# Linear attention and a multiplicative FFN on one core: the product with kv in quarters of the array

## The chip, the core and the metric

The kernel runs on one NeuronCore of a Trainium2 chip. TensorE (PE in the profile) multiplies: it holds a block of weights of up to 128 rows by 128 columns and streams the other operand through it, into PSUM, the accumulator memory. VectorE (DVE), ScalarE (ACT) and GpSimd (POOL) work on vectors; SyncE (SP) and POOL issue the DMAs. SBUF is the on-chip memory of 128 partitions.

The metric is the device time of one execution in microseconds (us), the median of several. An engine runs its own instructions in the order in which they were written; engines wait for each other by semaphores.

## The reference

For 8 batches and 8 heads, with 576 positions and 64 channels a head, the attention is linear; its result, with heads side by side as 512 channels, is the x of a feed-forward network on 4608 tokens.

```python
q_s = exp(q - max(q, -1)); q_s = q_s / (sum(q_s, -1) + 1e-09)
k_s = exp(k - max(k, 2));  k_s = k_s / (sum(k_s, 2) + 1e-09)
kv = einsum('bhsd,bhse->bhde', k_s, v)
attn = einsum('bhsd,bhde->bhse', q_s, kv)
x = attn.transpose(0, 2, 1, 3).reshape(4608, 512)
a = x @ w1                      # 512 x 1024
b = x @ w2
h = a * b @ w3                  # 1024 x 1024
out = h @ w_out                 # 1024 x 512
```

## The kernel before, in words

**Layout.** A partition holds a group g (0 or 1) of four heads and a block of 9 positions: partition g*64 + p has positions 9p to 9p+8 of heads 4g to 4g+3. Heads are handled in pairs: pair hp (0 or 1) of group g has the heads 4g+2hp and 4g+2hp+1, and i (0 or 1) tells them apart. 512 of the 576 positions of a batch (8 of each 9) are its main block, and make one chunk of the FFN; the remaining 64 positions of all 8 batches are collected in `xtail`, the ninth chunk.

**Attention of batch b.** The steps have these names: `kmx` (DVE, maximum of k over positions in a partition, L300 or the tree L306 to L311), `kmt` (TensorE transposes it, L317), `mx` (DVE, L322 and L324), `kmb` (TensorE transposes back, L332), `cb` (ACT copies it to SBUF, L337), `ksub` (L341, on POOL from batch 1 on), `kexp` (ACT, L349), `vc` (v to f16, L354), `kv` (TensorE, L365: 36 matmuls over 64 rows, g taking turns, with a column of ones that gives the sum of k). `kv2` (DVE, L372 to L376) takes the reciprocal of that sum and scales kv: the 128x128 product of a pair holds the two heads' kv on its diagonal 64x64 blocks and products of unlike heads off it, and a mask of ones and zeros, multiplied in, clears the latter. For q: `qmx` (DVE, L383), `qsub` (L387, POOL), `qexp` (ACT, L394), `qsm` (DVE, L400), `qeps` (ACT, L404), `qrc` (DVE, L408), `qn` (L413, POOL), `qt` (TensorE transposes, three groups of six, L422) and `qT` (ACT copies them to SBUF, L427). `xm` (L436) multiplies: for each pair and each g one full 128x128 by 128x512 matmul, into one PSUM tile; `xs` (ACT, L441) copies it to x, scaled. `xt` (L448) and `xts` (L453) do the same for the 64 tail positions, all four in one PSUM tile. The rows of x stand in the order pair, g, i; the loads of w1 and w2 pick their rows to fit.

**FFN of chunk c.** w3 is folded with w_out first (`w3t` L260, `w3T` L264, `pf` L269, `W3O` L273). Then for each of 8 blocks of 128 columns: `up` 1 and `up` 0 (TensorE, L531, four matmuls each, with w2 and with w1), `bs` (ACT, L537, copies the one out), `ab` (DVE, L542, multiplies the other with it). Four `down` (TensorE, L548, eight matmuls each) and `os` (ACT, L553) end the chunk, and SP stores it.

**What sets the order.** A planner (class `Plan`) does a list schedule when the kernel is built: each step has an engine, a length written by hand, the steps that it needs, and the PSUM or SBUF ring that it takes a buffer from; the planner always takes the step with the most work behind it among those that can start within 0.2 us. Its order is the order of the instructions. The rings: `pab` (4 PSUM banks, for `up`), `po` (2, for `down`), and `att` (2, for all of the attention: kmt, kmb, kv which takes both, qt, xm, xt). A step that takes a buffer waits for the evictions of the step that had it. `slack` adds 1 us to what a TensorE step of the attention assumes of its inputs.

**Loads.** SP loads k, q and v batch by batch, two buffers each; that of k of batch 1 waits for a load of w1 so that weights come first. POOL's queue loads the weights, converting them to f16.

The order of TensorE in the stretch that the prediction walks through is, before (batch numbers in brackets): `down`s of chunk 0, kv[1], down, qt[1] three times, kmt[2], xm[1] four times, kmb[2], then up 1 of chunk 1.

Of the kernel before, what the change touches and what calls it, by code (L numbers as in the profile page):

```python
# [9 lines left out]
F32 = mybir.dt.float32  # L10
# [113 lines left out]
def kernel(  # L124
# [15 lines left out]
    P = 128  # L140
# [31 lines left out]
    def p_att(shape, dtype, name):  # L172
        return att_pool.tile(shape, dtype, tag="att", name=name)
# [10 lines left out]
    ident16 = konst.tile([P, P], F16)  # L184
    ident32 = konst.tile([P, P], F32)
    epst = konst.tile([P, 1], F32)
    mask = konst.tile([P, P], F32)
    pace = konst.tile([P, 1], F32)
    make_identity(nc, ident16)
    make_identity(nc, ident32)  # L190
    dve.memset(epst, EPS)
    dve.memset(mask, 0.0)
    dve.memset(mask[0:64, 0:64], 1.0)
    dve.memset(mask[64:128, 64:128], 1.0)
    for t in v16buf:
        dve.memset(t[:, :, :, 128:129], 1.0)
    xtail = konst.tile([P, N_CT, B * HALF], F16)
# [38 lines left out]
    for n, which, dst in (("w2", moe_w2, w2sb), ("w1", moe_w1, w1sb)):  # L236
        for hp in range(NHP):
            for i in range(2):
                row = (4 * hp + 2 * i) * D
                w_load((n, hp, i), dst[i * HALF:(i + 1) * HALF, 2 * hp:2 * hp + 2, :],  # L240
                       which[row:row + 2 * D, :].rearrange("(g e) f -> e g f", g=G))

    def load(name, src, b, needs, after, wait):
        t = inbuf[name][b % 2]
# [39 lines left out]
    def attention(b):  # L284
# [84 lines left out]
        def kv2(gg):  # L369
            ps = st["pkv", b, gg]  # L370
            rc = work.tile([P, NHP], F32, tag="rc", name="rc")
            dve.tensor_scalar_add(out=rc, in0=ps[:, :, 128], scalar1=EPS)  # L372
            dve.reciprocal(out=rc, in_=rc)
            for hp in range(NHP):
                t = work.tile([P, P], F16, tag="kv2", name="kv2", bufs=8)
                dve.scalar_tensor_tensor(out=t, in0=ps[:, hp, 0:128], scalar=rc[:, hp:hp + 1],  # L376
                                         in1=mask, op0=ALU.mult, op1=ALU.mult)
                st["kv2", b, hp, gg] = t

        def qmx(hp):  # L380
            if ("qm", b) not in st:
# [46 lines left out]
                out=st["qT", b][:, n * BLK:(n + 1) * BLK, :, :].rearrange("p n g c -> p (n g c)"),  # L428
                in_=st["qtp", b, n].rearrange("p n c -> p (n c)"))

        def xm(hp, gg):
            ct = 2 * hp + gg
            if ("x", b) not in st:
                st["x", b] = work.tile([P, N_CT, MAIN], F16, tag="x", name="x", bufs=NX)
            st["px", b, ct] = p_att([P, NM, HALF], F32, "px")
            nc.tensor.matmul(st["px", b, ct], lhsT=st["kv2", b, hp, gg],  # L436
                             rhs=st["qT", b][:, hp * NJ:hp * NJ + NM, gg, :],
                             start=True, stop=True)

        def xs(ct):  # L440
            nc.scalar.mul(out=st["x", b][:, ct, :],  # L441
                          in_=st["px", b, ct].rearrange("p j c -> p (j c)"), mul=SC)

        def xt():
            st["pxt", b] = p_att([P, N_CT, HALF], F32, "pxt")
            for hp in range(NHP):
                for gg in range(G):
                    nc.tensor.matmul(st["pxt", b][:, 2 * hp + gg, :], lhsT=st["kv2", b, hp, gg],  # L448
                                     rhs=st["qT", b][:, hp * NJ + NM, gg, :],
                                     start=True, stop=True)  # L450

        def xts():
            nc.scalar.mul(out=xtail[:, :, b * HALF:(b + 1) * HALF], in_=st["pxt", b], mul=SC)  # L453

        def A(*a, **k):
            plan.add(*a, lead=LEAD, **k)
# [20 lines left out]
        A(("kv", b), "PE", 1.15, kv, [("kexp", b, hp) for hp in hps] +  # L477
          [("vc", b, hp) for hp in hps] + [("xt", b - 2)] * old, takes="att", slots=2, slack=SLACK)
        for gg in range(G):
            A(("kv2", b, gg), "DVE", 0.95, lambda gg=gg: kv2(gg),  # L480
              [("kv", b)], gives=[("kv", b)])
        for hp in hps:
            A(("qmx", b, hp), "DVE", 1.34, lambda hp=hp: qmx(hp), [("q", b)])
# [12 lines left out]
              [("xt", b - 2)] * old, takes="att", slack=SLACK)  # L496
            A(("qT", b, n), "ACT", 0.8, lambda n=n: qT(n), [("qt", b, n)], gives=[("qt", b, n)])
        for hp in hps:
            for gg in range(G):
                ct = 2 * hp + gg  # L500
                A(("xm", b, ct), "PE", 0.22, lambda hp=hp, gg=gg: xm(hp, gg),
                  [("kv2", b, gg)] + [("qT", b, n) for n in range((hp * NJ) // BLK,
                                                                   (hp * NJ + NM - 1) // BLK + 1)] +
                  [("up", 0, b - NX, N_FT - 1) for _ in range(1) if b >= NX], takes="att",
                  slack=SLACK)
                A(("xs", b, ct), "ACT", 0.6, lambda ct=ct: xs(ct), [("xm", b, ct)],
                  gives=[("xm", b, ct)])
        A(("xt", b), "PE", 0.2, xt, [("xm", b, ct) for ct in range(N_CT)], takes="att", slack=SLACK)
        A(("xts", b), "ACT", 0.4, xts, [("xt", b)], gives=[("xt", b)])

    NX = 3
    LEAD = 18.0
# [9 lines left out]
    def chunk(c):  # L522
        def x():
            return st["x", c] if c < B else xtail

        def up(fb, one):
            def mm():
                st["p", one, fb] = p_ab()
                w = (w1sb, w2sb)[one]
                for ct in range(N_CT):  # L530
                    nc.tensor.matmul(st["p", one, fb], lhsT=w[:, ct, fb * P:(fb + 1) * P],  # L531
                                     rhs=x()[:, ct, :], start=(ct == 0), stop=(ct == N_CT - 1))
# [12 lines left out]
        def down(tb):  # L545
            st["po", tb] = p_o()
            for ft in range(N_FT):
                nc.tensor.matmul(st["po", tb], lhsT=st["ab", c][:, ft, tb * P:(tb + 1) * P],  # L548
                                 rhs=W3O[:, ft, :], start=(ft == 0), stop=(ft == N_FT - 1))

        def os(tb):
            st["osb", tb] = work.tile([P, C], F32, tag="osb", name="osb", bufs=4)
            nc.scalar.copy(out=st["osb", tb], in_=st["po", tb])  # L553

        def store(tb):
            for i in range(2):
                b, j = (c, 2 * tb + i) if c < B else (2 * tb + i, NM)
                nc.sync.dma_start(
                    out=out[b * S:(b + 1) * S, :].rearrange("(p j) c -> p j c", j=NJ)[:, j, :],
                    in_=st["osb", tb][i * HALF:(i + 1) * HALF, :])  # L560

        A = plan.add
        xn = [("xs", c, ct) for ct in range(N_CT)] if c < B else [("xts", b) for b in range(B)]
# [58 lines left out]
```

## Time and profile before

| what | value |
| --- | --- |
| median of 3 runs | 269.18 us (268.92 to 270.15) |
| the profiled execution | 269.61 us, its span 267.8 us |
| TensorE busy | 241.6 us, 90% of the span |
| DVE, ACT, POOL busy | 156.1, 148.4, 118.1 us |
| up, down matmuls (L531, L548) | 150 and 65.6 us by length, 576 and 288 of them |
| xm, xt matmuls (L436, L448) | 32 and 32 of them |
| kv2's scaling (L376) | 32 of 346 ns on DVE |
| xs, xts (L441, L453) | 32 of 600 ns, 8 of 388 ns on ACT |
| granted TensorE clock, mean | 0.987 |

How to read it: the page gives busy time and shares for each engine, then 40 equal slices of the span with the busy share in tenths (and the clock that TensorE was granted), then the chain of work that ended last, followed back from the last instruction, and groups of instructions: line, engine, operation, output<-input, shapes, count | busy us, mean ns | idle time ahead of them and who ended it. A matmul's length in a record is its latency, and they overlap; the distance between starts tells the rate. The timeline lists merged instructions by start and length.

### The profile page before, as it was taken

The numbers are of one execution on the slowest core, as the hardware profiler recorded it, in microseconds if no ns is written. First come the engines' busy times: TensorE is split into PE (matmuls) and PEld (weight loads), VectorE is DVE, ScalarE is ACT, GpSimd is POOL, SyncE is SP. The second block draws the span as 40 slices with busy tenths as digits, with TensorE's granted clock in tenths as the row PEclk, the third lists the DMA queues.
The fourth block names the chain that finished last, engine by engine and source line by source line (L and its number), as shares of the span: only waits on it lengthen the run. The fifth ranks groups of instructions, "written<-read, shape, count | busy, mean of one in ns | idle before, by whom it ended". The sixth has DMA issues, their size and how long they took to land.

```text
span 267.8 us, 4026 instructions
## 1 busy us (share of the span) xinstructions
PE 241.6 (90%) x1520; PEld 121.3 (45%) x1520; DVE 156.1 (58%) x240; ACT 148.4 (55%) x241; POOL 118.1 (44%) x77
## 2 busy tenths in 40 slices
PE   0019999999699999999999999999999999999993
PEld 0008744445245545545544554455455544444441
DVE  1998237997877995595759739945223512312420
ACT  1171743684865688655855874685548444324321
POOL 1632000679699679807964990895025000000000
PEclk9999999999679999999999999999999999999999
DMA  7999999937912961495079429620060023014015
GB/s 251 335 210 211 210 255 397 391 116 229 387 73 67 402 180 39 157 396 135 2 281 316 93 78 401 160 50 2 16 141 0 2 67 92 1 41 116 1 38 121
DMA packets 20980, 43.26 MB, mean 162 GB/s; under 512 B 1760, under 2 KB 1760, under 8 KB 20960
## 3 DMA queue, kind: packets, MB, share of 16 engines
q1 hardware_dynamic: 18432, 37.75, 43.4%
q0 software_dynamic: 2528, 5.24, 10.4%
q8 instruction: 12, 0.20, 0.3%
q14 instruction: 8, 0.07, 0.1%
HBM read 38.80 MB, written 9.44 MB: 180 GB/s over the span
## 4 chain that ended last, share of the span: by engine, by line
PE 71%; DMA 13%; ACT 5%; POOL 4%; issue 3%; DVE 2%; SPq 0%; POOLq 0%; DVEq 0%; ACTq 0%
PE pab L531 39%; PE po L548 18%; DMA v<-in_v_dram 4%; PE po L269 4%; DMA w<-in_moe_w_dram 3%; DMA q<-in_q_dram 3%; PE pkv L365 3%; POOL k L341 3%; PE qtp L422 2%; PE px L436 2%; DMA k<-in_k_dram 2%; PE w3t L260 2%; ACT ek L349 1%; ACT eq L394 1%; POOL q L387 1%
## 5 line engine op out<-in xcount | busy, mean ns | idle before, releaser
L542 DVE TENSOR_TENSOR ab<-pab,bsb 128x512 f16<-128x512 f32 x72 | 49.5, 689 | 65.7 <-PE pab L531 58.8
L537 ACT CAST bsb<-pab 128x512 f16<-128x512 f32 x72 | 42.1, 585 | 51.1 <-PE pab L531 48.1
L531 PE MATMUL pab<-x,w2sb 128*128 128x512 f16 x256 | 66.8, 384 | 0.0
L531 PE MATMUL pab<-x,w1sb 128*128 128x512 f16 x256 | 66.7, 383 | 0.0
L548 PE MATMUL po<-W3O,ab 128*128 128x512 f16 x288 | 65.6, 379 | 0.0
L387 POOL TENSOR_TENSOR q<-q,qm 128x1152 f32<-128x1152 f32 x14 | 29.5, 2119 | 41.4 <-DVE qm L383 39.2
L341 POOL TENSOR_TENSOR k<-k,cb 128x1152 f32<-128x1152 f32 x14 | 36.6, 2632 | 17.4 <-issue 15.1
L531 PEld LDWEIGHTS <-w2sb 128*128 128x128 f16 x288 | 28.3, 99 | 32.5 <-issue 1.4
L548 PEld LDWEIGHTS <-ab 128*128 128x128 f16 x288 | 27.9, 98 | 32.4 <-issue 0.7
L531 PEld LDWEIGHTS <-w1sb 128*128 128x128 f16 x288 | 27.3, 99 | 30.8 <-issue 1.1
L553 ACT COPY osb<-po 128x512 f32<-128x512 f32 x36 | 21.0, 584 | 32.8 <-PE po L548 30.4
L413 POOL TENSOR_TENSOR en<-eq,qr 128x1152 f16<-128x1152 f16 x14 | 29.5, 2123 | 0.5 <-DVE qr L408 0.5
L300 DVE TENSOR_REDUCE km<-k 128x128 f32<-128x1152 f32 x12 | 25.7, 2146 | 1.8 <-DMA k<-in_k_dram 1.8
L400 DVE TENSOR_REDUCE qr<-eq 128x18 f32<-128x1152 f16 x16 | 21.4, 1345 | 1.7 <-ACT eq L394 1.5
L383 DVE TENSOR_REDUCE qm<-q 128x18 f32<-128x1152 f32 x16 | 21.0, 1337 | 0.4 <-DMA q<-in_q_dram 0.4
L349 ACT ACTIVATE ek<-k 128x1152 f16<-128x1152 f32 x16 | 18.7, 1167 | 2.4 <-POOL k L341 1.4
L394 ACT ACTIVATE eq<-q 128x1152 f16<-128x1152 f32 x16 | 18.6, 1166 | 2.0 <-POOL q L387 2.0
L427 ACT COPY qT<-qtp 128x768 f16<-128x768 f16 x24 | 18.7, 805 | 1.0 <-PE qtp L422 1.0
L441 ACT ACTIVATE x<-px 128x512 f16<-128x512 f32 x32 | 17.9, 600 | 2.1 <-PE px L436 2.0
L354 POOL CAST v<-v 128x1152 f16<-128x1152 f32 x12 | 13.5, 1147 | 8.9 <-DMA v<-in_v_dram 8.9
L269 PE MATMUL po<-wosb,w3T 128*128 128x512 f16 x64 | 15.0, 379 | 0.0
L436 PE MATMUL px<-qT,kv 128*128 128x512 f16 x32 | 11.1, 400 | 2.2 <-DVE mx L322 1.3
(52 smaller groups left out, 169.3 us busy)
## 6 DMA issues: line engine op xcount, KB each, us to landing
k<-in_k_dram SPq DMA_DIRECT2D x8, 1152.0 KB, 5.5
q<-in_q_dram SPq DMA_DIRECT2D x8, 1152.0 KB, 8.2
v<-in_v_dram SPq DMA_DIRECT2D x8, 1152.0 KB, 11.4
out_dram<-osb SPq DMA_DIRECT2D x72, 128.0 KB, 2.3
w<-in_moe_w_dram POOLq DMA_DIRECT2D x4, 512.0 KB, 12.0
wosb<-in_moe_w_out_dram POOLq DMA_DIRECT2D x2, 512.0 KB, 6.5
w2sb<-in_moe_w_dram POOLq DMA_DIRECT2D x4, 256.0 KB, 15.7
w1sb<-in_moe_w_dram POOLq DMA_DIRECT2D x4, 256.0 KB, 12.5
```

The costliest lines, as they stand in the source:

```text
L269: nc.tensor.matmul(st["pf", ft], lhsT=st["w3T", ft][:, gt, :], rhs=wosb[:, gt, :], start=(gt == 0), stop=(gt == N_FT - 1))
L300: dve.tensor_reduce(out=st["km", b][:, two(hp), :], in_=kb[:, two(hp), :, :].rearrange("p h j d -> p h d j"), axis=AX.X, op=ALU.max)
L341: TTK[b][hp][1].tensor_tensor(out=kb[:, two(hp), :, :], in0=kb[:, two(hp), :, :], in1=st["cb", b][:, two(hp), None, :].broadcast_to([P, 2, ...
L349: nc.scalar.activation(out=st["ek", b][:, hp, :, :].rearrange(flat, i=2), in_=kb[:, two(hp), :, :], func=AF.Exp)
L387: TTQ[b][hp][1].tensor_tensor(out=qb[:, two(hp), :, :], in0=qb[:, two(hp), :, :], in1=st["qm", b][:, two(hp), :, None].broadcast_to([P, 2, ...
L394: nc.scalar.activation(out=st["eq", b, hp], in_=qb[:, two(hp), :, :], func=AF.Exp)
L400: dve.tensor_reduce(out=rr, in_=st["eq", b, hp], axis=AX.X, op=ALU.add)
L413: TTN[b][hp][1].tensor_tensor(out=st["en", b][:, hp, :, :].rearrange(flat, i=2), in0=st["eq", b, hp], in1=st["qr", b][:, two(hp), :, None] ...
L531: nc.tensor.matmul(st["p", one, fb], lhsT=w[:, ct, fb * P:(fb + 1) * P], rhs=x()[:, ct, :], start=(ct == 0), stop=(ct == N_CT - 1))
L537: nc.scalar.copy(out=st["bsb", fb], in_=st["p", 1, fb])
L542: dve.tensor_tensor(out=st["ab", c][:, fb, :], in0=st["p", 0, fb], in1=st["bsb", fb], op=ALU.mult)
L548: nc.tensor.matmul(st["po", tb], lhsT=st["ab", c][:, ft, tb * P:(tb + 1) * P], rhs=W3O[:, ft, :], start=(ft == 0), stop=(ft == N_FT - 1))
```

## The change

The product with kv is no longer made of full 128x128 blocks with zeros off the diagonal. Each head's 64x64 block is multiplied alone, in a quarter of the array: rows i*64 on, columns g*64 on. The four heads of a pair index hp (two i, two g) so fill the four quarters, and a PSUM tile holds one i with both g, which is a plain order of channels. So x's row blocks are 2hp+i with g inside, and w1 and w2 are loaded in plain blocks of 128 rows (128 partitions of one row each, where it was 64 partitions of two). Nothing needs a mask any more: its three memsets go, and kv2 scales both pairs of a g in one DVE operation of 128x256. `xm` is now one step for a pair hp that takes two `att` buffers at once; `xt` takes two as well and is evicted by two `xts`. Each xm step has four matmuls of 64x64 by 64x512 (two steps a batch, where there were four of one full matmul), and xt has eight of 64 columns (four before). The planner's lengths for the changed steps are rewritten, so it makes a new order for all the engines.

In the order that results, TensorE has kmt, xm, xm, kmb and up in the same place of batch 1; ACT has both qexp of batch 2 between the qT of batch 1 and its first xs, where one of them stood behind the four xs before; POOL has the vc of batch 3 ahead of the ksub of batch 2; DVE has both kmx of batch 2 behind the last ab of chunk 0.

```diff
-    mask = konst.tile([P, P], F32)
-    dve.memset(mask, 0.0)
-    dve.memset(mask[0:64, 0:64], 1.0)
-    dve.memset(mask[64:128, 64:128], 1.0)
...
-                row = (4 * hp + 2 * i) * D
-                w_load((n, hp, i), dst[i * HALF:(i + 1) * HALF, 2 * hp:2 * hp + 2, :],
-                       which[row:row + 2 * D, :].rearrange("(g e) f -> e g f", g=G))
+                ct = 2 * hp + i
+                w_load((n, hp, i), dst[:, ct:ct + 1, :],
+                       which[ct * P:(ct + 1) * P, :].rearrange("(a p) f -> p a f", a=1))
...
-            for hp in range(NHP):
-                t = work.tile([P, P], F16, tag="kv2", name="kv2", bufs=8)
-                dve.scalar_tensor_tensor(out=t, in0=ps[:, hp, 0:128], scalar=rc[:, hp:hp + 1],
-                                         in1=mask, op0=ALU.mult, op1=ALU.mult)
-                st["kv2", b, hp, gg] = t
+            st["kv2", b, gg] = work.tile([P, NHP, P], F16, tag="kv2", name="kv2", bufs=4)
+            dve.tensor_tensor(out=st["kv2", b, gg], in0=ps[:, :, 0:128],
+                              in1=rc[:, :, None].broadcast_to([P, NHP, P]), op=ALU.mult)
...
-            st["px", b, ct] = p_att([P, NM, HALF], F32, "px")
-            nc.tensor.matmul(st["px", b, ct], lhsT=st["kv2", b, hp, gg],
-                             rhs=st["qT", b][:, hp * NJ:hp * NJ + NM, gg, :],
-                             start=True, stop=True)
+        def quarter(out, hp, i, gg, js):
+            rows, cols = slice(i * HALF, (i + 1) * HALF), slice(gg * HALF, (gg + 1) * HALF)
+            nc.tensor.matmul(out[cols], lhsT=st["kv2", b, gg][rows, hp, rows],
+                             rhs=st["qT", b][rows, hp * NJ + js.start:hp * NJ + js.stop, gg, :],
+                             start=True, stop=True)
+            for i in range(2):
+                st["px", b, 2 * hp + i] = p_att([P, NM, HALF], F32, "px")
+            for gg in range(G):
+                for i in range(2):
+                    quarter(st["px", b, 2 * hp + i], hp, i, gg, slice(0, NM))
...
-            st["pxt", b] = p_att([P, N_CT, HALF], F32, "pxt")
-                    nc.tensor.matmul(st["pxt", b][:, 2 * hp + gg, :], lhsT=st["kv2", b, hp, gg],
-                                     rhs=st["qT", b][:, hp * NJ + NM, gg, :],
-                                     start=True, stop=True)
-        def xts():
-            nc.scalar.mul(out=xtail[:, :, b * HALF:(b + 1) * HALF], in_=st["pxt", b], mul=SC)
+            for i in range(2):
+                st["pxt", b, i] = p_att([P, NHP, HALF], F32, "pxt")
+                    for i in range(2):
+                        quarter(st["pxt", b, i][:, hp:hp + 1, :], hp, i, gg, slice(NM, NJ))
+        def xts(i):
+            nc.scalar.mul(out=xtail[:, i::2, b * HALF:(b + 1) * HALF], in_=st["pxt", b, i], mul=SC)
...
-            A(("kv2", b, gg), "DVE", 0.95, lambda gg=gg: kv2(gg),
+            A(("kv2", b, gg), "DVE", 0.75, lambda gg=gg: kv2(gg),
...
-                A(("xm", b, ct), "PE", 0.22, lambda hp=hp, gg=gg: xm(hp, gg),
+            A(("xm", b, hp), "PE", 0.25, lambda hp=hp: xm(hp),
+              slots=2, slack=SLACK)
...
-        A(("xt", b), "PE", 0.2, xt, [("xm", b, ct) for ct in range(N_CT)], takes="att", slack=SLACK)
-        A(("xts", b), "ACT", 0.4, xts, [("xt", b)], gives=[("xt", b)])
+        A(("xt", b), "PE", 0.15, xt, [("xm", b, hp) for hp in hps], takes="att", slots=2,
+          slack=SLACK)
+        for i in range(2):
+            A(("xts", b, i), "ACT", 0.3, lambda i=i: xts(i), [("xt", b)], gives=[("xt", b)])
```

More of the change, by code (lines that the diff above doesn't have):

```diff
@@ L429, in qT, with xm @@
                 in_=st["qtp", b, n].rearrange("p n c -> p (n c)"))
-        def xm(hp, gg):
-            ct = 2 * hp + gg
+        def quarter(out, hp, i, gg, js):
[3 more added lines that the diff above has]
+                             start=True, stop=True)
+        def xm(hp):
             if ("x", b) not in st:
                 st["x", b] = work.tile([P, N_CT, MAIN], F16, tag="x", name="x", bufs=NX)
-            st["px", b, ct] = p_att([P, NM, HALF], F32, "px")
-            nc.tensor.matmul(st["px", b, ct], lhsT=st["kv2", b, hp, gg],
-                             rhs=st["qT", b][:, hp * NJ:hp * NJ + NM, gg, :],
-                             start=True, stop=True)
+            for i in range(2):
[3 more added lines that the diff above has]
+                    quarter(st["px", b, 2 * hp + i], hp, i, gg, slice(0, NM))
         def xs(ct):
@@ L498, in attention @@
         for hp in hps:
-            for gg in range(G):
-                ct = 2 * hp + gg
-                A(("xm", b, ct), "PE", 0.22, lambda hp=hp, gg=gg: xm(hp, gg),
[L502 to L507, printed above, removed]
-        A(("xt", b), "PE", 0.2, xt, [("xm", b, ct) for ct in range(N_CT)], takes="att", slack=SLACK)
-        A(("xts", b), "ACT", 0.4, xts, [("xt", b)], gives=[("xt", b)])
+            A(("xm", b, hp), "PE", 0.25, lambda hp=hp: xm(hp),
+              [("kv2", b, gg) for gg in range(G)] + [("qT", b, n) for n in range(
+                  (hp * NJ) // BLK, (hp * NJ + NM - 1) // BLK + 1)] +
+              [("up", 0, b - NX, N_FT - 1) for _ in range(1) if b >= NX], takes="att",
+              slots=2, slack=SLACK)
+            for i in range(2):
+                A(("xs", b, 2 * hp + i), "ACT", 0.6, lambda hp=hp, i=i: xs(2 * hp + i),
+                  [("xm", b, hp)], gives=[("xm", b, hp)])
+        A(("xt", b), "PE", 0.15, xt, [("xm", b, hp) for hp in hps], takes="att", slots=2,
+          slack=SLACK)
+        for i in range(2):
+            A(("xts", b, i), "ACT", 0.3, lambda i=i: xts(i), [("xt", b)], gives=[("xt", b)])
     NX = 3
@@ L562, in chunk @@
         A = plan.add
-        xn = [("xs", c, ct) for ct in range(N_CT)] if c < B else [("xts", b) for b in range(B)]
+        xn = [("xs", c, ct) for ct in range(N_CT)] if c < B else [("xts", b, i) for b in range(B) for i in range(2)]
         prev = [("down", c - 1, 3)] if c else []
```

## The prediction

> **What bounds the kernel now.** I read the page's busy shares first, then its slices, then the chain that ended last.
>
> ```profile
> PE 241.6 (90%) x1520; PEld 121.3 (45%) x1520; DVE 156.1 (58%) x240; ACT 148.4 (55%) x241; POOL 118.1 (44%) x77
> ...
> PEclk9999999999679999999999999999999999999999
> ```
>
> ```profile
> PE 71%; DMA 13%; ACT 5%; POOL 4%; issue 3%; DVE 2%; SPq 0%; POOLq 0%; DVEq 0%; ACTq 0%
> ```
>
> TensorE is the bound: from the first weight transpose at 19.98 us it works nearly without a gap to 263.44 us, and the chain is TensorE for 71%. So a microsecond saved on DVE, ScalarE or POOL buys nothing unless TensorE waits for it, and every microsecond added to TensorE's own row counts. The one bad place is in slices 10 and 11 (67 to 80 us), where the granted clock falls. The groups by form give the prices:
>
> ```profile
> L436 PE MATMUL px<-qT,kv 128*128 128x512 f16 x32 | 11.1, 400 | 2.2 <-DVE mx L322 1.3 <-ACT qT L427 0.3 <-ACT x L441 0.3
> ...
> L376 DVE SCALAR_TENSOR_TENSOR kv<-pkv,rc,mask 128x128 f16<-128x128 f32 x32 | 9.7, 346 | 0.6
> ...
> L453 ACT ACTIVATE xtail<-pxt 128x256 f16<-128x256 f32 x8 | 3.0, 388 | 0.3 <-PE pxt L448 0.3
> ```
>
> A matmul's 400 ns is its latency; in a stream they start 0.216 us apart (0.86 for four in the chain). The only operation of before that already works in a part of the array is the k-v product (64 rows by 128 columns). The timeline around one of them, start and length first:
>
> ```profile
> 182.92 1.03 PE L531 MATMUL pab<-x,w2sb 128*128 128x512 f16 x4
> ...
> 183.88 1.21 PE L365 MATMUL pkv<-v,ek 64*128 64x129 f16 x36
> ...
> 185.02 1.04 PE L531 MATMUL pab<-x,w1sb 128*128 128x512 f16 x4
> ```
>
> Four matmuls from 182.92 would let the next start at 183.78; pkv starts at 183.88, 0.10 late. Its 36 matmuls are 18 pairs; the last starts at 183.88 + 1.21 - 0.22 = 184.87, so a pair takes 0.99 / 17 = 0.058, while 129 columns alone in a 128x512 stream's rate would be 0.054. Two row halves thus run side by side. The next full-array matmul starts at 185.02, 0.15 after the last pair and not 0.058: 0.09 late. So going into a partial layout and back costs 0.10 + 0.09 = 0.19 us.
>
> **Product in quarters, xm (TensorE).** Before: 2 full matmuls per pair of heads, 2 x 0.216 = 0.43 us. After: 4 quarters of 64x64. If all four run side by side, a group is 0.19 + 0.216 + about 0.01 for the starts = 0.42. That is -0.01 x 16 groups = -0.2 us. No row shows two column halves at once, so both ends: four side by side and no switch cost, 0.23, gives -3.3; row pairs side by side and column halves in turn, 0.19 + 2 x 0.216 = 0.63, gives +3.2 (four in a row, 1.06, would be +10, but the pairs above exclude that for rows). I take -0.2, nearest to the pkv row, the only partial layout here.
>
> The Trainium skill bears on this. "TensorEngine Tiling (Array Packing)", Key Properties, lets 64x64 tiles work in parallel, but says that changing the tiling mode drains the engine; the trace agrees on the second with its 0.19 us. By the page's 4x speedup alone xm would be worth 16 x (0.43 - 0.22) = 3.4 us, an estimate; by the row it is worth 0.2. The same page says that column tiling loses the fast weight load, and "TensorE: Matmul & The Clock Gate", LDWEIGHTS, prices a load at columns / 1.2 ns; if three loads of 53 ns were exposed in each of 24 groups, that would add 3.8 us by estimate, and no run here shows it.
>
> **Tail product, xt (TensorE).** Before: 4 matmuls of 64 columns in 0.12 us (the chain's "PE pxt L448 x4"), 0.029 each. After: 8 quarters, two sets of four, 0.19 + 2 x 0.029 = 0.25. That is +0.13 x 8 = +1.1 us. Ends: no switch, 0.06, -0.5; all eight in turn, 0.42, +2.4. I take +1.1 by the same row.
>
> **Both att buffers at once.** The att PSUM ring has two buffers. xm now takes both, so a pair of heads waits for both evictions of whatever stood there, and xt as well. In most batches 1.7 us (a `down`) lies between the two xm, against two evictions of 0.60; that covers it, and if ScalarE were late by over 0.4 us the excess would be paid. Batch 1 has no cover. The order of TensorE there is qt 0-2, kmt of batch 2, xm, xm, kmb of batch 2, up, with nothing between. From the timelines of PE, ScalarE and DVE before:
>
> ```profile
> 70.30 1.01 PE L436 MATMUL px<-qT,kv 128*128 128x512 f16 x2 [1.33 <-DVE mx L322]
> ...
> 72.54 1.91 PE L531 MATMUL pab<-x,w2sb 128*128 128x512 f16 x4
> ```
>
> ```profile
> 68.42 1.18 ACT L394 ACTIVATE eq<-q 128x1152 f16<-128x1152 f32 x1
> 69.48 0.60 ACT L441 ACTIVATE x<-px 128x512 f16<-128x512 f32 x1
> ```
>
> ```profile
> 69.82 0.42 DVE L322 TENSOR_REDUCE mx<-kmt 128x4 f32<-128x256 f32 x1
> ```
>
> Before, the first px ran at 68.59 and ScalarE evicted it at 69.48, while TensorE waited for mx. I walk the changed order with the rows' lengths. Up to xt of batch 0 TensorE has the same steps (57.4). DVE now does kmx 1 (2.9) ahead of ab 1 and two qsm and a qmx ahead of the last ab of chunk 0, which ends at 59.5; down 0 wants it at 59.15: +0.35. kv 1 follows at 63.15, the last down ends at 66.05. DVE meanwhile does qmx 2 and both kmx 2 to 65.3, then the two kv2 (each 0.16 + 0.17 + about 0.43 and gaps = 0.85) to 67.0, against 65.93 before; the second qt waits for that. The three qT end at 69.3 on ScalarE. Next in its new order stand both qexp of batch 2, ahead of the first x eviction (before, one of them stood behind all four): the second needs POOL's qsub, done at 68.94, and ends at 71.6. xm 0 runs at 70.35, when mx frees kmt's buffer; evictions 71.6 to 72.8; only then xm 1, at half clock about 0.7 us, evictions from 73.75; kmb at 74.4 takes the first buffer free; up starts at 75.0, not 72.54: 2.45 later. But TensorE is at half clock there until about 76.4 (the starts 72.54, 74.24, 75.95 are 1.70 apart, not 0.86), so the work lost is (76.4 - 72.54) / 2 - (76.4 - 75.0) / 2 = 1.2 us. Ends: 0.3, if xm 1 finds its buffers near 72.0 as px did; 2.9, if the longer gap holds the clock down half as long again. (By the windows the mean clock is 0.90 over 52 to 74 us and 0.95 over 74 to 100: 4.4 + 2.6 = 7 us at half clock; 3.5 us more cost 1.7.) I take 1.2.
>
> **What the new order moves.** The planner's lengths changed, so each queue is reordered. SP's is the same. On POOL, v of batch 3 is converted ahead of ksub 2: its load leaves at 62.84 and takes 11.7, so it lands at 74.5, two casts of 1.15 end at 76.9, and ksub 2 starts there, not at 75.42. Behind it wait kexp 2 and kv 2; ksub ends at 82.1, kexp at 83.5, and TensorE reaches kv 2 after eleven groups, at about 85: covered by 1.5 us. In batch 2, os of down 0 now stands behind two qeps, which wait for qsm: about 0.4 us on the third down. In batch 3, qsm 4 stands ahead of the last ab, and xm 0 waits for mx of batch 4: 0.5 + 0.3. Before's own waits at 136 to 140 us (0.4) go. Sum +0.4 net with slack in places I could not place exactly; ends -0.6 (all covered, and before's waits gone) and +2.5.
>
> **kv2 in one operation, weights, the rest.** DVE: 32 of 346 ns become 16 of about 425 (the 128x256 f32 rows of DVE), and three memsets go: some 4 us less, hidden behind TensorE; were it on the path it could give at most 16 x 0.2 = 3 us, and the row of kv2's waiters shows 0.2. ScalarE: 8 tail evictions of 388 become 16 of about 0.28 (from 388 and 600 ns at 256 and 512 elements), +1.4 us at 55% busy; cover is the `up` that follows. w1 and w2: the same 8 transfers of 256 KB with 2 KB packets, in the same places of POOL's queue; zero, hidden by the fold's matmuls, which keep TensorE busy to 40 us; if they land 1 us later, up 0 waits by less, as one more fold product now stands ahead of it.
>
> **Sum.** -0.2 + 1.1 + 1.2 + 0.4 = +2.5 us on the profiled execution, 269.6 (span 267.8 and 1.8 around it), so 272.1. That execution lies 0.4 above the median of 269.18: 271.7.
>
> **Rivals.** (a) Column halves go in turn: +3.4 for xm and +0.5 for xt on top, 275.6; no row shows columns side by side, the pkv pairs speak for it only by likeness. (b) The switch costs nothing for quarters: 24 groups x 0.19 = 4.6 us back, so 267.1, faster. It decides once a switch is under about 0.09 us; all seven pkv of full clock show 0.19, against it. (c) The clock stays low one step longer after batch 1: +1.7, 273.4. (d) It makes no difference: batch 1 hides behind the wait for k's landing (67.65) and the xm is neutral, so only xt is left, about 270.3; against it, the ScalarE order above.
>
> **How the numbers follow.** Forecast 0.43, (c) 0.14, (a) 0.13, (b) 0.16, (d) 0.14. About 0.5%, 1.3 us, is what can be told from no change. Faster: (b) and a rest of the forecast's unplaced slack, 0.20. Same: (d) and the forecast's low edge, 0.17. Slower: 0.63. The range reaches from (b) to just past (a): 267 to 276.2; the forecast alone spans 270 to 274.
>
> **What would show it.** In the new profile: the four quarters of px starting some 4 ns apart and about 0.4 us from the matmul before a group to the one after; pxt groups near 0.25; up of chunk 1 starting about 75; and a gap of TensorE between 66 and 75 longer than before. Quarters 0.2 us apart mean (a); groups of 0.23 mean (b). I am wrong if the reordered batches 3 to 7 hold waits that I did not place.

## The result and the profile after

The changed kernel takes 272.08 us (median of 4 executions, 271.43 to 272.62), against 269.05 us for the kernel before beside it (4 executions, 268.06 to 270.15). The ratio is 1.0111, with an interval of 1.0065 to 1.0157: slower, by about 3 us. The profiled execution took 271.43 us, its span 269.3 us. A second set of executions of the same code, taken for the experiments (called after_again below), gave 272.21 us and the ratio 1.0127 [1.0096, 1.0159].

From the page of the kernel after, the busy time of the engines, the granted clock in 40 slices, and the shares of the chain that ended last:

```profile
PE 241.4 (90%) x1584; PEld 118.2 (44%) x1584; DVE 152.8 (57%) x221; ACT 148.7 (55%) x249; POOL 117.6 (44%) x77
...
PEclk9999999999899999999999999999999999999999
...
PE 84%; DMA 6%; POOL 4%; ACT 3%; issue 1%; SPq 0%; ACTq 0%
```

TensorE is the bound as before, with as much busy time; the total does not tell where the 3 us went. Three readings do: the cost of a group of quarters, the stretch of batch 1, and a stall in batch 3 that before did not have.

**A group of quarters.** Groups by form of the kernel after (engine, operation, shapes, count | busy us, mean ns | idle before them):

```profile
L428 PE MATMUL px<-qT,kv 64*64 64x512 f16 x64 | 7.3, 398 | 2.2 <-ACT x L442 1.3 <-DVE mx L318 0.5 <-ACT qT L421 0.3
...
L428 PE MATMUL pxt<-qT,kv 64*64 64x64 f16 x64 | 2.0, 203 | 0.0
```

The busy time of px fell from 11.1 to 7.3 us, which looks like a gain of 3.8 us. It is none: a record's length is latency, and the switch into and out of the quarters lies between the records. The timeline of TensorE shows it (start, length, operation, how many merged), once around an xm and once around an xt:

```profile
90.02 1.89 PE L550 MATMUL po<-W3O,ab 128*128 128x512 f16 x8
91.83 0.41 PE L428 MATMUL px<-qT,kv 64*64 64x512 f16 x4
92.18 1.90 PE L550 MATMUL po<-W3O,ab 128*128 128x512 f16 x8
...
175.62 1.03 PE L533 MATMUL pab<-x,w2sb 128*128 128x512 f16 x4
176.58 0.26 PE L428 MATMUL pxt<-qT,kv 64*64 64x64 f16 x8
176.76 1.04 PE L533 MATMUL pab<-x,w1sb 128*128 128x512 f16 x4
```

Eight full matmuls from 90.02, 0.216 apart, would let the next start at 91.75; the quarters start at 91.83, and the next full matmul at 92.18. So the four quarters occupy 92.18 - 91.75 = 0.43 us, as much as the two full matmuls before (2 x 0.216). In the single records of the trace the four start 3 to 4 ns apart, 0.093 us late, and the full matmul behind them starts 0.333 us after the last of them, of which 0.216 is that quarter's own slot: 0.117 late. All four do run side by side, and going in and out costs what that saves. The weight loads (PEld) show that the first quarter's weights are not loaded ahead:

```profile
90.45 0.96 PEld L550 LDWEIGHTS <-ab 128*128 128x128 f16 x5
91.83 0.11 PEld L428 LDWEIGHTS <-kv 64*64 64x64 f16 x4 [0.42 <-issue]
```

The load begins in the same 0.01 us as the quarter, after 0.42 us without a load; in the stream of full matmuls a load begins 0.21 us ahead of its matmul, after 0.12 us without one. The pkv of the kernel before at 183.88, which divides only the rows, shows the same 0.42. For xt, four full matmuls from 175.62 would end their slots at 176.48, and the next full matmul starts at 176.76: 0.28 us, where before's four took 0.12.

**Batch 1.** The kernel after: from the timelines of TensorE, ScalarE and DVE (in brackets the idle time ahead and who ended it).

```profile
68.14 0.37 PE L428 MATMUL px<-qT,kv 64*64 64x512 f16 x1 [0.26 <-ACT qT L421]
69.01 0.41 PE L428 MATMUL px<-qT,kv 64*64 64x512 f16 x3 [0.50 <-DVE mx L318]
70.74 0.89 PE L428 MATMUL px<-qT,kv 64*64 64x512 f16 x4 [1.32 <-ACT x L442]
72.32 0.69 PE L328 MATMUL kmb<-ident,mxe 128*128 128x128 f32 x2 [0.68 <-ACT x L442]
72.80 1.91 PE L533 MATMUL pab<-x,w2sb 128*128 128x512 f16 x4
```

```profile
67.96 2.24 ACT L388 ACTIVATE eq<-q 128x1152 f16<-128x1152 f32 x2
70.08 1.09 ACT L442 ACTIVATE x<-px 128x512 f16<-128x512 f32 x2
```

```profile
64.68 0.42 DVE L371 TENSOR_TENSOR kv<-pkv,rc 128x256 f16<-128x256 f32 x1
...
68.55 0.41 DVE L318 TENSOR_REDUCE mx<-kmt 128x4 f32<-128x256 f32 x1
```

Both qexp of batch 2 (two `eq`, 2.24 us) now stand ahead of the first x eviction, so the first two evictions come only at 70.08, and the second xm waits 1.32 us for them: the two buffers that it takes are the two that the first xm filled. The first quarter ran at 68.14, the other three had to wait for `mx`, which holds the second buffer. This is the chain that the prediction describes, 1.5 to 2.2 us earlier than it puts it.

**Batch 3.** Still the kernel after, TensorE, then POOL, then ScalarE:

```profile
103.72 1.03 PE L533 MATMUL pab<-x,w2sb 128*128 128x512 f16 x4
105.56 0.83 PE L416 MATMUL qtp<-ident,en 128*128 128x128 f16 x12 [0.82 <-ACT xtail L454]
...
107.09 1.03 PE L533 MATMUL pab<-x,w2sb 128*128 128x512 f16 x4
108.67 0.49 PE L416 MATMUL qtp<-ident,en 128*128 128x128 f16 x6 [0.55 <-ACT qT L421]
```

```profile
95.19 2.23 POOL L350 CAST v<-v 128x1152 f16<-128x1152 f32 x2 [5.88 <-DMA v<-in_v_dram]
97.39 4.20 POOL L407 TENSOR_TENSOR en<-eq,qr 128x1152 f16<-128x1152 f16 x2
101.54 2.12 POOL L381 TENSOR_TENSOR q<-q,qm 128x1152 f32<-128x1152 f32 x1
```

```profile
103.70 1.16 ACT L388 ACTIVATE eq<-q 128x1152 f16<-128x1152 f32 x1 [2.02 <-POOL q L381]
104.77 0.57 ACT L539 CAST bsb<-pab 128x512 f16<-128x512 f32 x1
105.23 0.45 ACT L454 ACTIVATE xtail<-pxt 128x128 f16<-128x128 f32 x2
```

POOL waits 5.88 us for the load of v of batch 4, because its conversion (vc 4) stands ahead of the qn of batch 3 in POOL's queue. qn 3 and the first qsub of batch 4 behind it are late; ScalarE waits 2.02 us for that qsub with a qexp of batch 4, and has the two tail evictions of xt queued behind; they hold both `att` buffers, and the qt of batch 3 on TensorE waits for one. By the starts, qt could have begun at 103.72 + 0.864 = 104.58: it is 0.98 late, and the third group at 108.67 another 0.71. No other engine had been slow; two casts stood in the wrong place of a queue that runs in order.

**The ledger.** The profiled executions of before and of after_again had the same mean granted clock, 0.987, so they can be set against each other line by line (269.61 and 272.11 us, spans 267.8 and 269.9). The starts of the first `up` of each chunk cut the span:

| stretch | before, us | after_again, us | difference | what is in it |
| --- | --- | --- | --- | --- |
| to chunk 0 | 36.22 | 36.12 | -0.10 | |
| chunk 0 to chunk 1 | 36.32 | 37.52 | +1.20 | batch 1, with one xt, 0.17 |
| chunk 1 | 25.98 | 25.27 | -0.71 | less of it at half clock |
| chunk 2 | 24.40 | 26.34 | +1.94 | qt late 0.71 + 0.71, xt 0.17, one kmb more, 0.22 |
| chunks 3 to 7 | 119.62 | 119.40 | -0.22 | six xt, about +1.0; one kmb less; small waits that before had, gone |
| the rest | 25.30 | 25.29 | -0.01 | |

The sum is +2.1 us of span. The other 0.4 of the 2.5 us between these two executions lies outside the span: the time exceeds the span by 1.77 us in the executions of before, and by 2.17 in those of after_again (medians).

### The profile page after: what moved, and what is told of

Same layout as the page of the kernel before. It is cut to its first block, busy times and chain, and to the rows that moved or that the text cites. A ratio compares the mean times of both kernels' runs of the same rounds, so it can differ in the third digit from the quotient of the medians.

```text
span 269.3 us, 4141 instructions
## 1 busy us (share of the span) xinstructions
PE 241.4 (90%) x1584; PEld 118.2 (44%) x1584; DVE 152.8 (57%) x221; ACT 148.7 (55%) x249; POOL 117.6 (44%) x77
## 4 chain that ended last, share of the span: by engine, by line
PE 84%; DMA 6%; POOL 4%; ACT 3%; issue 1%; SPq 0%; ACTq 0%
PE pab L533 44%; PE po L550 23%; PE po L265 5%; PE pkv L361 4%; DMA w<-in_moe_w_dram 3%; DMA q<-in_q_dram 3%; PE qtp L416 2%; PE w3t L256 2%; PE px L428 2%; POOL en L407 2%; POOL k L337 1%; ACT eq L388 1%; POOL q L381 1%; ACT qT L421 1%; PE kmb L328 1%
## 5 line engine op out<-in xcount | busy, mean ns | idle before, releaser
L550 PE MATMUL po<-W3O,ab 128*128 128x512 f16 x288 | 66.3, 379 | 0.0
L550 PEld LDWEIGHTS <-ab 128*128 128x128 f16 x288 | 27.2, 98 | 32.1 <-issue 2.0
L416 PE MATMUL qtp<-ident,en 128*128 128x128 f16 x144 | 10.6, 219 | 2.1 <-ACT qT L421 1.3
```

## The experiments

The kernels ran in three sets, each on one chip with its own executions of the kernel before; across sets the ratios to before are compared, and not the medians. Where an order is changed, the edit takes steps out of the planner's finished order and puts them back at another place, before the instructions are issued; nothing else moves. In the lists below a step is written as its name, batch and index.

**The changed kernel again.** The control for the others, with no edit.

> The changed kernel once more, as the control for the runs beside it. Theory (layout switches and order): 3.0 us over before, 272.1 by 269.1; the granted clock is halved for one or two steps of 3.4 us after batch 1, so single executions differ by up to 1.7 us. Rival (the new forms of the loads and of kv2): the same time, it can't be told apart here.

272.21 us (6 executions, 271.93 to 272.89) against 268.82 for before (11 executions), ratio 1.0127 [1.0096, 1.0159]. This and its ledger above are what the next kernels are compared with.

**The tail product in full matmuls.** xt alone goes back to four full matmuls.

```diff
-                    for i in range(2):
-                        quarter(st["pxt", b, i][:, hp:hp + 1, :], hp, i, gg, slice(NM, NJ))
+                    nc.tensor.matmul(st["pxt", b, gg][:, hp, :], lhsT=st["kv2", b, gg][:, hp, :],
+                                     rhs=st["qT", b][:, hp * NJ + NM, gg, :], start=True, stop=True)
```

> The tail product is done in four full 128x128 matmuls in place of eight quarters, with the same buffers, evictions and order; the tail positions so get products of unlike heads in another order and aren't the reference's. Theory (each excursion into the partial layout costs 0.19 us and the eight quarters 0.28 in all): 8 x (0.28 - 0.12) = 1.3 us less than the changed kernel. Rival (what it costs is the order alone): no difference, within 0.5 us.

271.71 us (271.15 to 272.28), ratio 1.0104 [1.0072, 1.0137]. The timeline of TensorE of this kernel around one xt:

```profile
177.04 1.03 PE L534 MATMUL pab<-x,w2sb 128*128 128x512 f16 x4
177.91 0.28 PE L450 MATMUL pxt<-qT,kv 128*128 128x64 f16 x4
178.02 1.03 PE L534 MATMUL pab<-x,w1sb 128*128 128x512 f16 x4
```

From the slot's end at 177.90 to 178.02 is 0.12 us, against 0.28 in quarters: 0.165 each by the single records (0.281 and 0.116), eight times 1.3 us of TensorE's row. Only 0.5 us of it shows in the median. Chunks 3 to 7, with six of the eight xt, are 0.9 us shorter than in after_again (118.51, 119.40). Where the rest went is not shown: px waited 1.4 us for mx (1.0 in after_again), and the qt of batch 3 were late by 0.98 + 0.71 (0.71 + 0.71), but the first trace of the kernel after has 0.98 + 0.71 as well, without the edit. The same edit is made again below, without the stall of batch 3.

**The conversion of v of batch 4 later.** Only the order is changed, on POOL.

```diff
-        for _, s in order:
-            s["emit"]()
+        seq = [s for _, s in order]
+        at = lambda n: next(i for i, s in enumerate(seq) if s["name"] == n)
+        for n in [("vc", 4, 1), ("vc", 4, 0)]:
+            s = seq.pop(at(n))
+            seq.insert(at(("qsub", 4, 1)) + 1, s)
+        for s in seq:
+            s["emit"]()
```

> POOL's two casts of v of batch 4 are moved behind the last qsub of batch 4; nothing else moves. Theory (POOL waits 5.9 us for that load, and through qsub, qexp and the tail's evictions on ScalarE the wait reaches TensorE's qt of batch 3): the two stalls of 0.98 and 0.71 us at 105 to 109 us go, 1.5 us less than the changed kernel. Rival (that stall is covered by slack that later steps give back, or a later wait takes its place): under 0.5 us less.

271.24 us (270.72 to 271.83), ratio 1.0088 [1.0054, 1.0123]: 1.0 less than the control. TensorE and POOL of this kernel at the same place:

```profile
105.89 0.83 PE L421 MATMUL qtp<-ident,en 128*128 128x128 f16 x12
...
108.29 0.50 PE L421 MATMUL qtp<-ident,en 128*128 128x128 f16 x6
```

```profile
96.35 4.20 POOL L412 TENSOR_TENSOR en<-eq,qr 128x1152 f16<-128x1152 f16 x2 [6.08 <-DVE qr L407]
...
109.82 2.24 POOL L355 CAST v<-v 128x1152 f16<-128x1152 f32 x2
```

Neither qt waits any more, and chunk 2 takes 24.92 us instead of 26.34. POOL still idles 6 us, now for DVE, but nothing that TensorE needs soon is behind it. So the chain from POOL's queue to the qt is shown, and it was worth 1.0 us of the time and 1.4 of that chunk.

**Weights and kv2 as before.** The loads of w1 and w2 go back to 64 partitions of two rows, and kv2 to one scaling for each pair with the mask, whose three memsets return; the quarters stay.

```diff
-                w_load((n, hp, i), dst[:, ct:ct + 1, :],
-                       which[ct * P:(ct + 1) * P, :].rearrange("(a p) f -> p a f", a=1))
+                w_load((n, hp, i), dst[i * HALF:(i + 1) * HALF, 2 * hp:2 * hp + 2, :],
+                       which[2 * hp * P:2 * (hp + 1) * P, :].rearrange(
+                           "(a h p) f -> h p a f", a=2, h=2)[i])
...
-            dve.tensor_tensor(out=st["kv2", b, gg], in0=ps[:, :, 0:128],
-                              in1=rc[:, :, None].broadcast_to([P, NHP, P]), op=ALU.mult)
+            for hp in range(NHP):
+                dve.scalar_tensor_tensor(out=st["kv2", b, gg][:, hp, :], in0=ps[:, hp, 0:128],
+                                         scalar=rc[:, hp:hp + 1], in1=mask,
+                                         op0=ALU.mult, op1=ALU.mult)
```

> Two parts of the change are undone: w1 and w2 are loaded in 64 partitions of two rows each, and kv2 scales each pair of heads in an operation of its own with the mask; x's order, the quarters and the order of all steps stay. Theory: no difference from the changed kernel, within 0.5 us; DVE's work is some 3 us longer and hidden. Rival (the new forms cost or save time): it goes back towards before by 1 us or more, or on from it.

272.48 us (271.91 to 272.57), ratio 1.0129 [1.0098, 1.0159], which can't be told from the control. In the sum these parts cost nothing, as the prediction has it. But the time outside the span is 1.79 us here, as in before, and not 2.17, while the spans are 0.6 us longer than the control's (medians 270.65 and 270.05). So the 0.4 us outside the span belong to one of these parts; what they are, and why the span grew, stays open.

**One qexp of batch 2 behind the x evictions.** On ScalarE `("qexp", 2, 1)` goes behind `("xs", 1, 3)`, as before had it, and on DVE `("qsm", 2, 1)`, which needs it, follows.

```diff
+        for n in [("qexp", 2, 1)]:
+            s = seq.pop(at(n))
+            seq.insert(at(("xs", 1, 3)) + 1, s)
+        for n in [("qsm", 2, 1)]:
+            s = seq.pop(at(n))
+            seq.insert(at(("qexp", 2, 1)) + 1, s)
```

> On ScalarE the second qexp of batch 2 is moved behind the four evictions of x of batch 1 (its qsm follows it on DVE, whose order stays). Theory (that qexp, ahead of the evictions, holds both att buffers and so the second xm): the first eviction ends about 0.6 us earlier and chunk 1 starts that much earlier; at half clock there, 0.3 to 0.6 us less than the changed kernel's 272.2. Rival (the wait for the maximum, which stands behind the landing of k of batch 3, sets it): no difference.

271.97 us (4 executions, 271.90 to 272.57), ratio 1.0115 [1.0071, 1.0159]: little or nothing. Chunk 1 starts at 73.11, 0.5 earlier than in the control, but TensorE's waits in this kernel (us in total, times, longest) read:

```profile
PE px L436 <- DVE mx L326: 1.0, 1, 1.0
...
PE px L436 <- ACT x L450: 0.7, 1, 0.7
...
PE pab L541 <- ACT bsb L547: 0.2, 1, 0.2
```

```profile
79.09 1.17 ACT L353 ACTIVATE ek<-k 128x1152 f16<-128x1152 f32 x1 [1.28 <-POOL k L345]
```

With ScalarE's order mended, px still waits for mx on DVE, which stands behind a `kmx` that waits for the load of k of batch 3. The short wait of `up` for bsb, at 80.78, is not the moved qexp's: the eviction stands behind this kexp of batch 2, which waits for POOL's ksub. The order of ScalarE was one of two waits in that place, and taking one away left the other.

**The kernel before again, and with its mx moved.** The second has the one edit that takes the other wait away in the kernel before: on DVE the first half of the `kmx` of batch 3, which waits for its load, goes behind the mx of batch 2.

```diff
+        for n in [("kmx", 3, 0)]:
+            s = seq.pop(at(n))
+            seq.insert(at(("mx", 2)) + 1, s)
```

> The kernel before once more, for a second trace of it. All theories: 268.8 us, waits of about 4.4 us in batch 1's stretch from 65 to 73 us, and 1 us of small waits between 130 and 166.

> In the kernel before, DVE's maximum of k of batch 3 (which waits for that load) is moved behind mx of batch 2, which frees a buffer that xm of batch 1 waits for. Theory (the two att buffers are what batch 1 waits for): the second px starts about 1.4 us earlier, 1 us less than before, 267.8; the clock may also come back a step earlier. Rival (ScalarE's evictions set the stretch): no difference.

Before again: 268.29 us (10 executions, 266.99 to 270.38), ratio 0.9988 [0.9949, 1.0028]. With mx moved: 267.82 (10 executions, 266.77 to 269.11), ratio 0.9970 [0.9938, 1.0003]. The timeline of TensorE of the latter:

```profile
67.35 0.63 PE L441 MATMUL px<-qT,kv 128*128 128x512 f16 x2 [0.27 <-ACT qT L432]
68.89 0.87 PE L441 MATMUL px<-qT,kv 128*128 128x512 f16 x2 [0.92 <-ACT x L446]
...
70.22 1.79 PE L536 MATMUL pab<-x,w2sb 128*128 128x512 f16 x4
```

Chunk 1 starts at 70.22, which is 35.25 us after chunk 0; it was 36.32 in the kernel before. That gives the lowest median and ratio of all kernels run here, though its interval still touches 1.

**All three moves in the changed kernel.** vc 4, kmx 3 and qexp 2 moved as above, and the quarters of an xm issued tile by tile (`i` outside, `gg` inside). Of these four edits vc 4 and qexp 2 were also run alone in the changed kernel; the other two were not.

```diff
-            for gg in range(G):
-                for i in range(2):
+            for i in range(2):
+                for gg in range(G):
```

> The changed kernel with three moves (casts of v of batch 4 behind the last qsub, the second qexp behind the evictions of x of batch 1, the maximum of k of batch 3 behind mx of batch 2), and xm's quarters issued tile by tile, so that the first two need one buffer only. Theory (order and the both-buffers wait cost 2 to 2.5 us of the 3.1, the tail product the rest): 1.0 + 0.4 + 0.6 less, 270.0 to 270.4, still above before. Rival (the quarters are what costs): 271 or more.

270.66 us (10 executions, 270.21 to 271.12), ratio 1.0070 [1.0050, 1.0089]. Chunk 1 starts 35.46 us after chunk 0 (37.52 in the control), 2.1 us won. But a new stall took part of it. TensorE, POOL and ScalarE of this kernel:

```profile
80.41 1.02 PE L547 MATMUL pab<-x,w1sb 128*128 128x512 f16 x4 [1.46 <-ACT bsb L553]
```

```profile
73.86 2.24 POOL L364 CAST v<-v 128x1152 f16<-128x1152 f32 x2 [3.71 <-DMA v<-in_v_dram]
76.05 5.21 POOL L351 TENSOR_TENSOR k<-k,cb 128x1152 f32<-128x1152 f32 x2
```

```profile
78.72 1.16 ACT L359 ACTIVATE ek<-k 128x1152 f16<-128x1152 f32 x1 [2.08 <-POOL k L351]
79.79 1.05 ACT L553 CAST bsb<-pab 128x512 f16<-128x512 f32 x2
```

The same pattern a batch earlier: vc 3 waits 3.71 us for its load, ahead of the ksub of batch 2; kexp 2 waits for that on ScalarE, and the evictions of `up` stand behind it. In the changed kernel as it is, this wait is there too (3.35 us, ksub at 75.76) and costs nothing, because batch 1 is late by more. The lateness of one stretch was the cover of a wait in the next.

**And vc of batch 3 moved.** The same with `("vc", 3, 1)` and `("vc", 3, 0)` behind `("qsub", 3, 1)`.

```diff
+        for n in [("vc", 3, 1), ("vc", 3, 0)]:
+            s = seq.pop(at(n))
+            seq.insert(at(("qsub", 3, 1)) + 1, s)
```

> The three moves and the tile-by-tile quarters, and POOL's two casts of v of batch 3 moved behind the last qsub of batch 3. Theory (with batch 1 shortened, POOL's wait of 3.7 us for that load has lost its cover and stops TensorE for 1.5 us at 80 us): that stall goes, 1.0 to 1.5 us less than the 270.7 of the run before, 269.2 to 269.7. Rival (another wait takes its place): 270.3 or more.

268.82 us (12 executions, 268.49 to 270.38), ratio 1.0013 [0.9988, 1.0037]. The longest of TensorE's waits from batch 1 on in this kernel; two of 0.2 us follow them:

```profile
PE px L445 <- ACT x L459: 0.9, 1, 0.9
PE qtp L433 <- ACT qT L438: 0.7, 1, 0.7
PE px L445 <- ACT qT L438: 0.3, 1, 0.3
```

From a ratio of 1.0127 to 1.0013, about 3 us, with the quarters, the wide kv2 and the plain rows all still there: a better order of the same instructions gives back nearly all that the change lost. One of the four moves, that of mx, is not the changed kernel's own loss, since the kernel before starts chunk 1 earlier by it as well.

**The two products in full matmuls, on that order.** xt back to four full matmuls (the diff above), and in another kernel xm back to two for each pair.

```diff
-            for i in range(2):
-                for gg in range(G):
-                    quarter(st["px", b, 2 * hp + i], hp, i, gg, slice(0, NM))
+            for gg in range(G):
+                nc.tensor.matmul(st["px", b, 2 * hp + gg], lhsT=st["kv2", b, gg][:, hp, :],
+                                 rhs=st["qT", b][:, hp * NJ:hp * NJ + NM, gg, :],
+                                 start=True, stop=True)
```

> The kernel of the run beside it, with the tail product in four full matmuls (tail positions aren't the reference's). Theory (0.165 us for each of 8 tail products, all on TensorE's row now that the order leaves few waits): 1.0 to 1.3 us less than the run beside it, so at or just below before. Rival (only half is to be had, as in the first such run): 0.6 us or less.

> The same again, with xm in two full matmuls in place of four quarters (x gets products of unlike heads and isn't the reference's; the tail is in quarters). Theory (a group of quarters takes 0.436 us of TensorE with its two switches, two full matmuls 0.431): no difference from the first run of this call, within 0.4 us. Rival (the quarters cost or gain beside the row that the trace shows): 1 us or more either way.

| kernel, on the mended order | us | ratio to before |
| --- | --- | --- |
| xm and xt in quarters | 268.82 (268.49 to 270.38) | 1.0013 [0.9988, 1.0037] |
| xt in full matmuls | 267.95 (267.36 to 269.57) | 0.9993 [0.9967, 1.0020] |
| xm in full matmuls | 268.94 (268.24 to 269.73) | 1.0008 [0.9984, 1.0031] |
| the kernel before with mx moved | 267.82 (266.77 to 269.11) | 0.9970 [0.9938, 1.0003] |

Quarters of xt cost 0.9 us of the median, and 0.9 to 1.1 between executions of like clock (269.39 and 270.25 at a mean clock of 0.987, 267.71 and 268.80 above it): most of the 1.3 us of the row. For xm the medians show nothing, but they mix clocks: seven of twelve executions with full matmuls had a mean clock of 0.999 or 1.000, two of twelve with quarters. Between executions at 0.991 and 0.992 full matmuls took 268.38 us (four, 268.24 to 268.43) and quarters 268.73 (eight, 268.49 to 269.02), so quarters of xm cost about 0.3 us there, somewhat more than the 0.1 of TensorE's row; the rest of it is not explained. No kernel with quarters beat the kernel before clear of the noise.

## Why the prediction was right or wrong

The forecast was +2.5 us on the profiled execution and 271.7 us; between profiled executions of equal clock the difference is 272.11 - 269.61 = +2.5, and the median came to 272.08, 3.0 above the 269.05 beside it. The sum holds, in part by luck: batch 1 came out 0.7 us smaller than its term, 0.4 us came outside the span, where no term looks, and two of the four terms are made of other things than it says.

**xm, -0.2 us: right in mechanism, and near in size.** The group was put at 0.42, it measures 0.436 by the single records, against 0.431 for two full matmuls: +0.1 us over 16 groups. The switch that the pkv row showed at 0.10 + 0.09 is 0.093 + 0.117 for quarters. The Trainium skill's "TensorEngine Tiling (Array Packing)", Key Properties, says that tiles run in parallel and that a change of mode drains the array. The runs agree with the first by the starts 3 to 4 ns apart, and with the second by the 0.21 us, as large as the gain; that it is a drain is not shown. The page's Restrictions have column tiling lose the fast weight load. The first quarter's weights are loaded late here, but the pkv, which leaves the columns whole, shows the same gap of 0.42 us ahead of its loads and a switch of 0.19 us, so only 0.02 us of the switch is seen with quarters alone.

**xt, +1.1 us: right.** 0.281 against 0.116 is +0.165 for each of eight, +1.3 us, a little more than predicted, since the eight quarters start over 63 ns (3 to 4 ns apart, and 43 ns between the two sets) and not over 29. Removing it gave 0.5 us in the changed kernel and 0.9 on the mended order.

**Batch 1, +1.2 us net: the right mechanism, oversized.** Chunk 1 started 1.2 us later against chunk 0 (1.20 in after_again, 0.9 in after), where 2.45 was forecast, and after the half clock's share the net is some +0.5 (+1.20 - 0.71 in the ledger, one xt included). The term that was too large is the walk of DVE: it put the end of chunk 0's last ab at 59.5 and that of the last kv2 at 67.0, with a down waiting 0.35 us for DVE on the way; the ab ended at 57.7 and the kv2 at 65.1 in the kernel after, and no down waited. Everything behind moved up with it: the second qexp ended at 70.2 and not 71.6. What the walk says of the order, both qexp ahead of the evictions and the second xm behind these, stands in the profile line by line.

**What the new order moves, +0.4 us: wrong in its places.** Of the waits listed there, neither the third down behind os nor xm 0 of batch 3 behind mx shows in the waits of TensorE. The step failed by what it does not list: vc 4 ahead of qn 3 on POOL, a 5.9 us wait for a load, 1.4 to 1.7 us on TensorE, in the same batch and by the pattern that the step itself describes for vc 3. Its size came out near only because before's own small waits between 130 and 166 us, about 1.2 us, went as well, of which it foresaw 0.4. For vc 3 it was right (ksub at 75.76, one microsecond sooner than put, and covered), and all_moves showed how thin that cover is.

**kv2, weights, tail evictions, nothing: right for the sum.** With the first two undone the time was the same, though it was divided differently between the span and what lies outside it; the tail evictions were not undone alone.

**The rivals.** (a), column halves in turn, is excluded by the starts of the quarters. (b), a free switch, is excluded by the 0.21 us of a group. (d), no difference, is excluded by the time; its argument, that batch 1 is hidden, holds in part, since batch 1 cost less than forecast. (c), one more step of low clock, did not come as a new length: the longer of before's two lengths came more often, as told below.

## What to carry to other kernels

Before packing the array, set the time saved in one excursion into the packed layout against one switch: here 0.216 us saved against 0.21 us paid, so four quarters of 512 columns came out nearly even and those of 64 columns lost. A planner that orders the queues makes every change of a length or of a buffer count a new kernel: look in each in-order queue for an instruction that waits for a load with other work behind it, since setting three such places right, with one on ScalarE and the order of the quarters, gave back about 3 us here, and undoing the changed tail product about one. And when a stretch gets shorter, ask which wait its lateness had been hiding.

## What the runs showed of the hardware that was not expected

The fall of the clock near 70 us comes in steps. The windows of before, and then of the kernel after (in each line the window, its length, busy time of the engines, and third from the end the granted clock):

```profile
66.00:70.00 4.00, 1.80 (x18) 1.06 (x16) 2.26 (x2) 4.00 (x6) 4.00 (x4) 0.95 1.06 408
70.00:74.00 4.00, 3.44 (x9) 1.28 (x9) 3.97 (x5) 2.82 (x5) 1.76 (x3) 0.50 1.03 372
74.00:78.00 4.00, 4.00 (x15) 1.56 (x13) 2.42 (x3) 1.75 (x5) 4.00 (x2) 0.70 0.23 88
```

```profile
70.00:74.00 4.00, 2.46 (x9) 1.09 (x9) 4.00 (x4) 2.92 (x7) 0.65 (x2) 0.71 1.01 356
74.00:78.00 4.00, 4.00 (x17) 1.73 (x16) 3.42 (x6) 1.48 (x3) 4.00 (x3) 0.86 0.02 8
```

At half clock for a share s, a window of 4 us has the mean 1 - s / 2, so before was low for 2 x 4 x (0.05 + 0.50 + 0.30) = 6.8 us, after for 2 x 4 x (0.29 + 0.14) = 3.4. The records give 6.83 and 3.41 (6.83 again in after_again), and where a trace had such a stretch near 70 us it was one of these two lengths. The executions of a kernel fall into groups by their mean clock: of 65 of the kernel before, run beside the experiments, 28 had up to 0.987, with a median of 269.5 us, and 37 had 0.990 or more, with 268.07. Of ten of the changed kernel eight were in the lower group (272.28) and two in the upper (271.43 and 271.93), and of twelve on the mended order two. So among executions of like clock the change costs 2.8 us in the lower group and about 3.6, from two executions, in the upper; the counts suggest that the order also changes how often the longer stretch comes. More clock was not always less time: with xm in full matmuls on the mended order, the executions at 0.992 took 268.24 to 268.43 us and those at 0.999 or 1.000 took 268.48 to 269.31. The trace of that kernel, at full clock from 24 to 266 us, has a wait of 1.7 us of `up` for bsb that all_moves_vc3, with 6.83 us at half clock, does not have. What brings the fall, and what decides its length, stays open: from 66 to 70 us TensorE was busy for 1.80 of 4 us in before, which fell, and for 1.90 in that trace, which did not.
